# A gated recurrence and a SwiGLU block on one core: two units' decayed k turned through DRAM, sign passes moved between two engines, two outputs on another queue

## The chip, the core and the metric

The kernel runs on one core of one Trainium2 chip. Its engines are TensorE (PE in the profile; PEld is its weight load), VectorE (DVE), ScalarE (ACT), GpSimd (POOL) and SyncE (SP). SyncE, GpSimd and ScalarE can issue DMAs: those of SyncE stand in queue q1, those of GpSimd in q0, those of ScalarE in q10. The metric is the device time of one execution in microseconds, lower being better.

## What is computed

An outer-product recurrence with a decay per channel (4 sequences, 8 heads, 768 steps, 48 channels), whose output is the input of a gated feed-forward block with 384 model and 1536 hidden channels. Cut to what matters:

```python
f = 1.0 / (1.0 + np.exp(-f_logit))
for t in range(S):
    state = f[:, :, t, :, None] * state + np.einsum('bhd,bhe->bhde', k[:, :, t], v[:, :, t])
    y[:, :, t] = np.einsum('bhd,bhde->bhe', q[:, :, t], state)
x = y.transpose(0, 2, 1, 3).reshape(B * S, H * D)
g = x @ w_gate
out = (g * (1.0 / (1.0 + np.exp(-g))) * (x @ w_val)) @ w_out
```

The weights are handed in as 64-bit floats, which the kernel turns into 32-bit ones on the chip.

## The kernel before

**Units and chunks.** Each sequence is cut into 6 chunks of 128 steps. A unit is one chunk of one sequence. Units are numbered chunk by chunk, so that units 0 to 3 are the first chunk (c = 0), 4 to 7 the second, and 8 to 11 the third (c = 2). `attention(u)` is a generator that does one unit, a step at each `next`. After a chunk's four units comes that chunk's feed-forward block. The code runs the block of chunk c while the attention of chunk c + 1 is done.

**One unit.** Sigmoid of f (L619 and L626); f is turned so that channels lie on partitions (L614 by TensorE in the first chunk, L630 by VectorE later); the same for k (L641); `tail`, the decay from a step to the chunk's end, by a scan (L651); the decayed k, kT = k times tail (L593); `gate`, the decay from the start, by a second scan (L681); q turned (L685); qT (L593 again); the scores sc (L700) of kT and qT on TensorE; the mask A (L719) by VectorE; then y (L742 and L746, or L767 with the last sequence) and the chunk's contribution dS (L787) to the state. dS needs the decayed k with the steps on partitions, called kt. There are two ways to it. In one, TensorE transposes kT (L704) and ScalarE copies the result out of PSUM (L717). In the other ("turned"), VectorE transposes blocks of 32 by 32 into the room in which k was loaded (L668), four DMAs write these to DRAM (`turn`, L671), and one DMA reads them back in another order (L709 or L715). In that case the next unit's k (L449), which is loaded into the same room, is asked for only after the turns. Each of its four DMAs fills 32 partitions. In the line of `turned`, the third chunk's first two units go the first way, and the other two the second.

**The blocks.** Chunk 0's block is plain (`mlp_plain`: L836 for gate and val, L859 for the last product). The others (`mlp_fifteen`) take fifteen products (L1052) in place of eighteen in each of four triples, on sums of weights (L951, L954) and of tokens, and seven in place of eight in the last product (L1151, L1214). Each product's accumulator in PSUM is read on the way by ScalarE (`c` or `aside`, L1057) and VectorE (c plus or minus aside or o). Banks named o and c share two buffers, which are also where the second and third unit's scores lie from the third chunk on. The sums of the last product's weights are DMAs that add in flight: ScalarE writes a negated copy (L991), and GpSimd adds to it (L992).

**Weights.** `weight_piece` fetches a piece (L474 by SyncE). ScalarE makes `up` from the low word (L491) and `top` from the high one (L495). VectorE clamps `top` (L505), shifts it and adds (L510 or L516; L502 in the very first, whose two halves are called separately). The sign bits come in one of two ways. For pieces listed in `SIGNED`, ScalarE writes them by a further pass L494, and VectorE shifts only (L508). For the others VectorE shifts and masks (L512) and writes the signs (L514). The first two pieces (gate and val of the first hidden columns) are cut in two halves.

**Order.** The order on TensorE, VectorE, ScalarE and SyncE is written out by hand and pinned by `in_order`; from the third chunk on GpSimd's too. Tables of times (`EARLY`, `CHAINS`, `SCORES`, `JOINS_AT`, `SIZES_AT`, `FETCHES_AT`, `SUMS_AT`, `DOWN_SUMS_AT`) say at which point of the block's products each step of a unit, a piece or a sum is put into that order. An engine takes its instructions strictly in this order: one that waits holds all behind it.

```python
turned = SQUARES * B + 2 <= u < (NCH - 1) * B or c < SQUARES and in_squares
at_once = turned and c >= SQUARES and b < B - 1
```

Here SQUARES is 2 and B is 4, so that the first line begins at unit 10.

Of the kernel before, what the change touches and what calls it, by code (L numbers as in the profile page):

```python
# [290 lines left out]
def short_path(ctx, tc, ident, least, judge, q, k, v, f_logit, moe_w_gate, moe_w_val, moe_w_out, out):  # L291
# [9 lines left out]
    nc = tc.nc  # L301
    B, H, S, D = q.shape
    C = 128
    NCH = S // C
# [11 lines left out]
    SQUARES = 2  # L316
# [86 lines left out]
    def by_squares(u):  # L403
        return u >= SQUARES * B - 3
# [124 lines left out]
    NW = 2  # L529
    FIRST = 2  # L530
    NPART = 2
    SIGNED = (4, 6, 7, 8, 9, 11, 15, 16, 17)

    def add_piece(dst, src, parts=1):
        fetch, *rest = weight_piece(dst, src, parts, len(fetches) in SIGNED)
        fetches.append(fetch)
        for group, fs in zip((sizes, joins), rest):
            group += fs
# [37 lines left out]
    def attention(u):  # L576
        b, c = units[u]
# [7 lines left out]
        in_squares = by_squares(u)  # L585
# [45 lines left out]
            load_after(u, "f")  # L631
        yield

        turned = SQUARES * B + 2 <= u < (NCH - 1) * B or c < SQUARES and in_squares
        turn_queue = nc.sync if c >= SQUARES else nc.gpsimd
        kT = att.tile([128, HP, C], FP32, tag="kT", name="kT")
        qT = att.tile([128, HP, C], FP32, tag="qT", name="qT", bufs=2)
# [8 lines left out]
        n = HP * N1  # L646
# [83 lines left out]
        if c and b < B - 1:  # L730
# [20 lines left out]
            for h in range(H):  # L751
                a, par = h // 2, h % 2
                f = h * D
                while f < (h + 1) * D:
                    n = min((h + 1) * D, (f // 128 + 1) * 128) - f
# [74 lines left out]
    def mlp_plain(c):  # L830
        h = {}

        def product(w, j, name):
            p = fps.tile([128, 512], FP32, tag="m", name=name)[:, 0:TB]
            for i in range(KT):
                nc.tensor.matmul(p, lhsT=w[:, j, i, :], rhs=xT[c][:, i, :],  # L836
                                 start=(i == 0), stop=(i == KT - 1))
            return p

        def part(j):  # L840
            k = 2 * (j // NP)
            return hidden_tile(h, j % NP)[:, k:k + 2, :].rearrange("p a t -> p (a t)")

        def gate(j):
            p = product(w_gate, j, "gate")
            lag(nc.scalar.activation, part(j), p, AF.Silu)

        def val(j):
            p = product(w_val, j, "val")
            lag(nc.vector.tensor_tensor, part(j), part(j), p, ALU.mult)  # L850

        return [*[(PLAIN, lambda j=j, f=f: f(j)) for f, j in ((gate, 0), (val, 0), (gate, 1), (val, 1))],
                *[(PLAIN, lambda j=j, f=f: f(j)) for i in range(2, NF, 2) for f in (gate, val) for j in (i, i + 1)],
                *[(PLAIN_DOWN, f) for f in downs_abreast(c, h)]]
# [48 lines left out]
    def chain(k, q, qmul, turn=None, head=None):  # L903
        return (*[k + t for t in STEPS], turn or k + 3.5, head or k + 3.5, q, qmul)
# [6 lines left out]
        ((PRODUCT - 0.05, "b"), (between[1], "o"), (between[3], "o"), (down[3], "A")),  # L911
        *[((down[10] - whole, "A"), (between[1], "o"), (between[3], "o"), (down[3], "A"))] * (NCH - 4)))}
    CHAINS = {c: chains for c, chains in zip(range(2, NCH), (
        (chain(2.6, 4, 8.6), chain(14.5, 20, 23), chain(30, 37, 43.2), chain(57.4, 57.8, 61)),
        (chain(-12, -8.5, -5), chain(3.5, 6, 9), chain(16, 28, 33, 21.5, 23.5), chain(40.1, 53, 55, 44.5, 52)),
        *[(chain(-19.4, -11.2, -9.5), (-7.5, -6.3, 1.3, 2.2, 3.2, 5.5, 8, 10), chain(16, 28, 33, 21.5, 23.5), chain(40.1, 53, 55, 44.5, 52))] * (NCH - 4)))}
    LAST = 72.5
# [9 lines left out]
    def score_bank(u):  # L927
# [3 lines left out]
            return bank("sc")  # L931
        return {"o": banks_o, "A": banks_a}[kind].tile([128, 512], FP32, tag=kind, name="sc")

    JOINS_AT = (0.8, 4.5, 5, 7.6, 13.2, 16.3, 20.3, 27.2, 29.6, 36.1, 38.7, 43.3, 46.6, 47.8, 55.3, 55.4, 67.6, 70.8)
    SIZES_AT = (0.39, 2.4, 6.2, 11.1, 13.2, 18.4, 18.6, 22.1, 31.8, 38, 39.8, 40.1, 43.1, 50.8, 53, 56, 64.8)
    FETCHES_AT = (-1.1, 0.6, 5.5, 5.9, 6, 9.2, 10.6, 21.1, 23.6, 27, 35.5, 35.5, 37.8, 42.4)
    EARLY = (
        (-1.01, 4.17, 4.58, 9.7, 9.87, 10.5, 11, 11.5, 12, 13.4, 17.3, 22, 28.4, 28.41, 33),
        (26, 31.3, 32.8, 34.3, 34.6, 34.6, 36.1, 37.4, 38.2, 40.6, 43.3, 43.4, 50.8, 54.81, 56),
        (46.2, 49.2, 50.7, 51.4, 51.5, 57, 57.6, 58, 62, 63.9, 64.4, 65.5, 68.2, 68.21, 70),  # L940
        (63, 64, 66.8, 66.9, 67.4, 67.9, 68.6, 71.6, 73.3, 75.9, 76, 76.7, 78, 78.41, 80.3))
    SUMS_AT = (64.3, 64.5, 72.58, 72.7, 74.06, 74.74, 75.3, 75.42, 75.98, 76.02, 76.18, 76.3, 76.66, 76.86,
        77.34, 77.54, 78.22, 78.5, 79.18, 79.86, 81.22, 81.26, 81.26, 81.34, 81.62, 81.9, 81.94, 82.58, 82.58, 82.7,
        83.2)
    LATE_SUMS_AT = (23,)
    FINISH = (3, 5, 6, 7, 9, 10)
    DOWN_SUMS_AT = (5.2, 5.21, 18.8, 18.81, 34.5, 34.51, 43, 43.01)
    sums = {}

    def plus(dst, a, b):  # L950
# [31 lines left out]
    def down_weight_sums():  # L982

        DH = DM // 2
        b11, b12 = w_out[:, 0:NP, 0:DH], w_out[:, 0:NP, DH:DM]
        b21, b22 = w_out[:, NP:NF, 0:DH], w_out[:, NP:NF, DH:DM]
        for i in (1, 2, 4):
            down_sums[i] = comb.tile([128, NP, DH], FP32, tag=f"ws{i}", name=f"ws{i}")
        return [f for dst, a, b in ((down_sums[1], b12, b11), (down_sums[2], b22, down_sums[1]), (b12, b22, b12),
                                    (down_sums[4], b21, down_sums[2]))  # L990
                for f in (lambda dst=dst, b=b: nc.scalar.mul(dst, b, -1.0),  # L991
                          lambda dst=dst, a=a: nc.gpsimd.dma_start(out=dst, in_=a, accum_op=ALU.add))]  # L992
# [10 lines left out]
    def lag(f, *args):  # L1003
        lagging.append(lambda: f(*args))  # L1004
# [123 lines left out]
    def down_seven(c, h):  # L1128
# [15 lines left out]
        def bank2(name, tag):  # L1144
            pool = {"A": banks_a, "B": banks_b, "o": banks_o}[tag]
            return pool.tile([128, 512], FP32, tag=tag, name=name)[:, 0:DM].rearrange("p (n d) -> p n d", n=2)

        def add(p, lhsTs, rhs, first, part):
            for j in order[part * NP // 2:(part + 1) * NP // 2]:
                for n in range(2):  # L1150
                    nc.tensor.matmul(p[:, n, :], lhsT=lhsTs[j][:, n * C:(n + 1) * C], rhs=rhs[:, j, :],  # L1151
                                     start=first and j == order[0] and n == 0, stop=j == order[-1],
                                     skip_group_check=True)

        def of_h(k):
            return [hidden_tile(h, j)[:, k, :] for j in range(NP)]
# [38 lines left out]
        def five(part):  # L1195
            if part == 0:
                kept["p"] = bank2("o7", "o")
            add(kept["p"], of_h(1), b12, True, part)
            if part:
                lag(plus, kept["u"], kept["u"], kept["p"])  # L1200
                lag(plus, kept["o", 1][:, :, DH:DM], kept["u"], kept["p5"])
                lag(plus, kept["o", 1][:, :, 0:DH], kept["u"], kept["p4"])
                for n in range(2):
                    lag(put_out, 1, n, nc.scalar)

        def six(part):
            if part == 0:
# [14 lines left out]
    def in_turn_of_time(waiting, steps):  # L1222

        waiting.sort(key=lambda x: x[0])
        now = 0.0

        def come_in():
            while waiting and waiting[0][0] <= now:
                waiting.pop(0)[1]()

        come_in()
        for took, f in steps:
            come_in()
            before = lagging[:]
            lagging.clear()
            f()
            for g in before:
                g()
            now += took
        come_in()  # L1240
        for g in lagging:
            g()
        lagging.clear()
        assert not waiting
# [4 lines left out]
    mark = traced[-1]  # L1249
    keep_warm(5)  # L1250
    first = [attention(b) for b in range(B)]
    done = [0] * B

    def run(b, *steps):
        for s in steps:
            assert done[b] == s
            done[b] += 1
            for _ in range((3, 1, 5, 3, 3)[s]):
                next(first[b])
# [23 lines left out]
            sizes.pop(0)()  # L1283
        run(b - 1, 4)
    first_join = joins.pop(0)
    first_join(("clamp"))
    sizes.pop(0)()
    run(B - 1, 3)
    first_join(("add"))
    joins.pop(0)()  # L1290
    next(first[B - 1])
    sizes.pop(0)()
# [2 lines left out]

    waiting = [(t, sizes.pop(0)) for t in SIZES_AT]
    waiting += [(t, joins.pop(0)) for t in JOINS_AT]
    waiting += [(t, fetches.pop(0)) for t in FETCHES_AT]
    assert not fetches and not sizes and not joins
    waiting.append((-0.02, lambda: sigmoid_ahead(B)))  # L1300
    for b, at in enumerate(EARLY):
        run_of = attention(B + b)
        waiting += [(t, lambda run_of=run_of: next(run_of)) for t in at]
    sums_of = [weight_sums(odd) for odd in range(2)]
    sums = sums_of[0][0:7] + sums_of[1][0:7] + sums_of[0][7:] + sums_of[1][7:]
    waiting += zip(SUMS_AT, sums[:len(SUMS_AT)])
    in_turn_of_time(waiting, mlp_plain(0))
# [22 lines left out]

    assert len(SUMS_AT) + len(LATE_SUMS_AT) == len(sums)
    waiting += zip(LATE_SUMS_AT, sums[len(SUMS_AT):])
    waiting += [(at, f) for at, f in zip(DOWN_SUMS_AT, down_weight_sums())]
    blocks = {}
# [16 lines left out]
def kernel(  # L1351
# [22 lines left out]
    def judge(bank):  # L1374
# [13 lines left out]
        yield  # L1388

    short_path(tc, ident, least, judge, *args)  # L1390
    with tc.If(redo[0] > 0, label="redo"):
        general_path(tc, *args)
# [32 lines left out]
```

## Time and profile before

| | us |
|---|---|
| Median of 3 runs | 597.67 (597.44 to 597.67) |
| The profiled execution | 597.51 |
| Its span, first to last instruction | 595.8 |
| TensorE busy | 585.5 |
| VectorE busy | 479.3 |
| ScalarE busy | 301.1 |
| GpSimd busy | 112.8 |

The span of the profiled execution leaves out 1.7 us around it. The granted clock of TensorE was 1.0 throughout. The page's slices show where the engines are full: each digit is the busy share of a fortieth of the span, 9 being 90% or more.

```profile
PE   7899999999999999999999999999999999999996
PEld 4744444667888999888999888899988899988896
DVE  7997998999989877998986888994978972666741
ACT  3488677025877322676640667632476730356600
```

VectorE is nearly full in the first third, where it also turns the weights into 32-bit floats and forms their sums. A row of a timeline gives start, duration, engine, line, operation, the tiles written and read, their shapes and the count. What stands in brackets is the idle time before it and what ended that.

### The profile page before, as it was taken

The page shows a single profiled execution, that of the slowest core. Times are in us where ns is not written, and L with a number is a line of the kernel's source. Part 1 is how long each engine was busy: PE and PEld are TensorE (multiplying, and loading weights), DVE is VectorE, ACT ScalarE, POOL GpSimd, SP SyncE. Part 2 cuts the span into 40 slices and gives each one's busy share as a digit, 9 for nine tenths or more (in the row PEclk, how much of TensorE's full clock was granted, in tenths as well). Part 3 has the DMA queues.
Part 4 walks back from the last instruction along what each step waited for, and adds up shares of the span by engine and source line. Part 5 has one row for each costly group of instructions (what it writes and reads, how often), then busy time and mean ns, then how long its engine had stood idle before and what let it go on. Part 6 is the DMA issues. An engine that isn't in the chain of part 4 may idle for free.

```text
span 595.8 us, 10874 instructions
## 1 busy us (share of the span) xinstructions
PE 585.5 (98%) x3972; PEld 481.8 (81%) x3972; DVE 479.3 (80%) x830; ACT 301.1 (51%) x563; POOL 112.8 (19%) x240
## 2 busy tenths in 40 slices
PE   7899999999999999999999999999999999999996
PEld 4744444667888999888999888899988899988896
DVE  7997998999989877998986888994978972666741
ACT  3488677025877322676640667632476730356600
POOL 3140345202132330212030030330030330000000
PEclk9999999999999999999999999999999999999999
DMA  9999487233666565542345332543231100100001
GB/s 205 253 307 286 142 217 186 60 98 107 122 117 110 96 150 136 138 100 64 84 117 137 99 80 62 112 111 99 74 99 28 29 10 6 53 2 1 2 1 56
DMA packets 106291, 61.86 MB, mean 104 GB/s; under 512 B 64200, under 2 KB 97032, under 8 KB 106232
## 3 DMA queue, kind: packets, MB, share of 16 engines
q1 hardware_dynamic: 93800, 45.96, 31.0%
q0 software_dynamic: 10992, 13.19, 10.0%
q10 hardware_dynamic: 1440, 1.97, 0.9%
q8 instruction: 32, 0.52, 0.4%
q14 instruction: 27, 0.22, 0.1%
HBM read 47.64 MB, written 8.13 MB: 94 GB/s over the span
## 4 chain that ended last, share of the span: by engine, by line
PE 98%; DVE 1%; ACT 0%; issue 0%; DVEq 0%
PE o L1151 20%; PE A L1052 18%; PE B L1052 15%; PE c L1052 6%; PE o L1052 6%; PE o L859 5%; PE gate L836 5%; PE val L836 5%; PE sc L700 4%; PE o L1214 3%; PE y L746 3%; PE y L767 2%; PE dS L787 2%; PE y L742 2%; PE kt L704 1%; PE fTp L614 0%
## 5 line engine op out<-in xcount | busy, mean ns | idle before, releaser
L757 POOL DMA_DIRECT2D xT<-yT x120 | 59.8, 506 | 53.4 <-ACT yT L750 49.0
L1052 PE MATMUL A<-xs,w_both 128*128 128x256 f32 x240 | 62.2, 382 | 0.0
L1151 PE MATMUL o<-w_out,h 128*128 128x192 f32 x360 | 62.0, 327 | 0.0
L1151 PEld LDWEIGHTS o<-w_out,h 128*128 128x128 f32 x360 | 58.7, 190 | 1.0 <-issue 0.2
L1057 ACT COPY c<-A 128x512 f32<-128x512 f32 x40 | 23.3, 583 | 60.5 <-PE A L1052 59.4
L1057 ACT COPY aside<-A 128x512 f32<-128x512 f32 x60 | 35.2, 586 | 32.9 <-PE A L1052 32.7
L951 DVE TENSOR_TENSOR c<-c,aside 128x512 f32<-128x512 f32 x60 | 41.1, 685 | 12.8 <-ACT aside L1057 11.1
L1052 PEld LDWEIGHTS A<-xs,w_both 128*128 128x128 f32 x240 | 44.9, 190 | 6.6
L1004 DVE TENSOR_TENSOR h<-h,c 128x256 f32<-128x256 f32 x100 | 40.6, 414 | 7.6 <-ACT h L1068 7.3
L954 DVE TENSOR_TENSOR c<-c,aside 128x512 f32<-128x512 f32 x60 | 41.0, 684 | 2.7 <-ACT aside L1057 2.7
L1068 ACT ACTIVATE h<-c 128x256 f32<-128x256 f32 x100 | 39.4, 417 | 5.0 <-DVE c L951 3.8
L719 DVE TENSOR_TENSOR A<-sc,causal 128x512 f32<-128x512 f32 x48 | 30.9, 685 | 13.4 <-PE sc L700 13.4
L1151 PE MATMUL o<-ws,h 128*128 128x192 f32 x240 | 41.5, 328 | 0.0
L1052 PE MATMUL B<-xs,w_both 128*128 128x256 f32 x160 | 41.3, 380 | 0.0
L1052 PE MATMUL A<-xs,extra 128*128 128x256 f32 x160 | 41.2, 380 | 0.0
L1052 PE MATMUL c<-xT,w_both 128*128 128x256 f32 x160 | 41.1, 379 | 0.0
L1052 PE MATMUL B<-xT,extra 128*128 128x256 f32 x160 | 41.0, 379 | 0.0
L1057 ACT COPY aside<-B 128x512 f32<-128x512 f32 x60 | 35.2, 586 | 9.0 <-PE B L1052 7.0
L1151 PEld LDWEIGHTS o<-ws,h 128*128 128x128 f32 x240 | 39.1, 190 | 0.5
L954 DVE TENSOR_TENSOR c<-o,c 128x512 f32<-128x512 f32 x40 | 27.4, 686 | 11.0 <-ACT h L1068 6.2
L951 DVE TENSOR_TENSOR c<-c,o 128x384 f32<-128x384 f32 x15 | 8.2, 548 | 34.8 <-PE o L1151 34.8
L690 POOL MEMSET gates<- 128x4 f32 x24 | 3.6, 150 | 169.0 <-DVE qT L593 163.9
(163 smaller groups left out, 1240.2 us busy)
## 6 DMA issues: line engine op xcount, KB each, us to landing
fsquares<-in_f_logit_dram SPq DMA_DIRECT2D x64, 96.0 KB, 4.1
qsquares<-in_q_dram SPq DMA_DIRECT2D x64, 96.0 KB, 2.3
ksquares<-in_k_dram SPq DMA_DIRECT2D x64, 96.0 KB, 2.4
w<-in_moe_w_gate_dram SPq DMA_DIRECT2D x6, 768.0 KB
w<-in_moe_w_val_dram SPq DMA_DIRECT2D x6, 768.0 KB, 6.5
w<-in_moe_w_out_dram SPq DMA_DIRECT2D x6, 768.0 KB, 8.8
v<-in_v_dram SPq DMA_DIRECT2D x19, 192.0 KB, 2.8
turn<-ksquares SPq DMA_DIRECT2D x40, 64.0 KB, 2.2
```

The source lines that it names most:

```text
L700: nc.tensor.matmul(sc[par][:, a * C:(a + 1) * C], lhsT=kT[r, a, :], rhs=qT[r, a, :], start=True, stop=True)
L719: nc.vector.tensor_tensor(A[:, par], sc[par].rearrange("p (a t) -> p a t", t=C), causal.unsqueeze(1).broadcast_to((128, HP, C)), ALU.mult)
L757: (nc.gpsimd if c >= SQUARES else nc.sync).dma_start(out=xT[c][f % 128:f % 128 + n, f // 128, b * C:(b + 1) * C], in_=yT[r:r + n, par, a / ...
L836: nc.tensor.matmul(p, lhsT=w[:, j, i, :], rhs=xT[c][:, i, :], start=(i == 0), stop=(i == KT - 1))
L859: nc.tensor.matmul(p, lhsT=hidden_tile(h, n // 2)[:, n % 2 * 2 + b // 2, b % 2 * C:(b % 2 + 1) * C], rhs=w_out[:, j, :], start=(n == 0), s ...
L951: nc.vector.tensor_tensor(dst, a, b, ALU.add)
L954: nc.vector.tensor_tensor(dst, a, b, ALU.subtract)
L1004: lagging.append(lambda: f(*args))
L1052: nc.tensor.matmul(p[name][:, n, :], lhsT=weights_of[a][:, n, j, :], rhs=tokens[b], start=fresh and n == 0, stop=True, skip_group_check=True)
L1057: nc.scalar.copy(t, p[name])
L1068: nc.scalar.activation(dst, src[:, 0, :], AF.Silu)
L1151: nc.tensor.matmul(p[:, n, :], lhsT=lhsTs[j][:, n * C:(n + 1) * C], rhs=rhs[:, j, :], start=first and j == order[0] and n == 0, stop=j == ...
```

## The change

Four things change.

1. Units 8 and 9 go the turned way too: `turned` begins at SQUARES * B. TensorE's L704 and ScalarE's L717 go for both, and VectorE's L668, four DMAs L671 and one read L709 come for each. The loads of k for units 9 and 10 come after the turns of the unit before.
2. `SIGNED` takes in pieces 0 and 1 in place of 4 and 8.
3. The first block of the fifteen-product kind (c = 1) issues its second pair of outputs (`put_out`, L1160) on GpSimd's queue in place of ScalarE's.
4. The tables of times are set anew for the first and second chunk's weight pieces, sums and units, for the third chunk's chains, and for the second pair of the adding DMAs (18.8 becomes 20.7).

The brackets around "clamp" and "add" make tuples of them; the same instructions come out.

```diff
-    SIGNED = (4, 6, 7, 8, 9, 11, 15, 16, 17)
+    SIGNED = (0, 1, 6, 7, 9, 11, 15, 16, 17)
...
-        turned = SQUARES * B + 2 <= u < (NCH - 1) * B or c < SQUARES and in_squares
+        turned = SQUARES * B <= u < (NCH - 1) * B or c < SQUARES and in_squares
...
-        (chain(2.6, 4, 8.6), chain(14.5, 20, 23), chain(30, 37, 43.2), chain(57.4, 57.8, 61)),
+        (chain(2.6, 4.8, 8.6), chain(14.5, 21.7, 23.2, 21.2, 19.6), chain(30, 37, 43.6), chain(57.4, 56.6, 61)),
...
-    JOINS_AT = (0.8, 4.5, 5, 7.6, 13.2, 16.3, 20.3, 27.2, 29.6, 36.1, 38.7, 43.3, 46.6, 47.8, 55.3, 55.4, 67.6, 70.8)
+    JOINS_AT = (0.8, 3.3, 5, 7.6, 12.8, 15.9, 19.9, 22.6, 25.2, 34.9, 38.3, 42.9, 46.6, 48.2, 56.1, 56.2, 67.6, 70.8)
...
-        (-1.01, 4.17, 4.58, 9.7, 9.87, 10.5, 11, 11.5, 12, 13.4, 17.3, 22, 28.4, 28.41, 33),
+        (-1.01, 4.17, 4.58, 9.7, 9.8, 9.87, 11.3, 11.8, 12.3, 14.2, 17.3, 22, 31.4, 31.41, 34.8),
...
-    DOWN_SUMS_AT = (5.2, 5.21, 18.8, 18.81, 34.5, 34.51, 43, 43.01)
+    DOWN_SUMS_AT = (5.2, 5.21, 20.7, 20.71, 34.5, 34.51, 43, 43.01)
...
-                    lag(put_out, 1, n, nc.scalar)
+                    lag(put_out, 1, n, nc.gpsimd if c == 1 else nc.scalar)
...
-    first_join(("clamp"))
+    first_join(("clamp",))
```

## The prediction

> **What bounds the kernel now.** I read the page's chain first, then the waits of TensorE, then the timeline of each engine in three stretches: 22 to 31 us (where TensorE still waits), 28 to 140 us, and 138 to 235 us (the third chunk's attention).
>
> ```profile
> PE 98%; DVE 1%; ACT 0%; issue 0%; DVEq 0%
> ...
> PE idle L362 <- DVE floor L354: 2.1, 1, 2.1
> PE sc L700 <- DVE qT L593: 1.6, 2, 0.8
> ```
>
> The chain that ended last is TensorE for 98% of the span, and what TensorE waits for in the waits view adds up to some 5 us, all of it before 25.3 us. From 29.6 us to the end its starts follow each other without a hole over 0.12 us. So a microsecond can be won in two ways only: by taking matmuls away, or in the opening. It can be lost wherever a wait for TensorE newly appears.
>
> The opening. VectorE clears weights between the last unit's qT and its mask A, and A opens the way to y, xT and the first product:
>
> ```profile
> 25.12 0.70 DVE L505 TENSOR_SCALAR top<-top 128x384 f32<-128x384 f32 x1
> 25.85 0.36 DVE L512 TENSOR_SCALAR top<-top 128x384 int32<-128x384 int32 x1
> 26.13 0.59 DVE L514 TENSOR_SCALAR up<-w 128x384 uint16<-128x384 uint16 x1
> 26.60 1.28 DVE L719 TENSOR_TENSOR A<-sc,causal 128x512 f32<-128x512 f32 x2
> ...
> 25.25 1.16 PE L700 MATMUL sc<-qT,kT 48*128 48x128 f32 x16 [0.79 <-DVE qT L593]
> ```
>
> The transposes to be removed, and for comparison a score step that has none after it:
>
> ```profile
> 150.62 1.16 PE L700 MATMUL sc<-qT,kT 48*128 48x128 f32 x16
> 151.72 0.65 PE L704 MATMUL kt<-idf,kT 128*128 128x128 f32 x4
> 152.21 1.03 PE L1052 MATMUL A<-xT,w_both 128*128 128x256 f32 x4
> ...
> 75.74 1.16 PE L700 MATMUL sc<-qT,kT 48*128 48x128 f32 x16
> 76.83 5.42 PE L836 MATMUL gate<-xT,w_both 128*128 128x512 f32 x12
> ```
>
> VectorE in the third chunk, which has almost no hole from 140 to 169 us: the first unit's kT, the second's k transpose, and the operation that frees the bank which the second unit's scores need.
>
> ```profile
> 144.07 0.66 DVE L593 TENSOR_TENSOR kT<-qT,tails 128x512 f32<-128x512 f32 x1
> ...
> 155.75 0.71 DVE L641 STREAM_TRANSPOSE qT<-ksquares 128x512 f32<-128x512 f32 x1
> ...
> 167.02 0.67 DVE L954 TENSOR_TENSOR c<-c,c 128x512 f32<-128x512 f32 x1
> ...
> 168.73 1.16 PE L700 MATMUL sc<-qT,kT 48*128 48x128 f32 x16
> ```
>
> Last, the DMA queues. The third unit of the chunk already goes through DRAM: its four turn writes, then the next k load, which overwrites what the turns read. GpSimd starts an adding DMA (L992, 576 KB) beside it.
>
> ```profile
> 181.27 2.64 SPq L671 DMA_DIRECT2D turn<-ksquares  x4
> 184.01 6.33 SPq L449 DMA_DIRECT2D ksquares<-in_k_dram  x4
> ...
> 146.64 1.50 POOL L992 DMA_DIRECT2D ws<-w_out  x1 [5.57 <-ACT ws L991]
> 148.50 3.67 SPq L449 DMA_DIRECT2D qsquares<-in_q_dram  x4
> ```
>
> The load that takes 1.8 us to issue elsewhere took 6.33 us. The DMA view of 149 to 152.5 us says why: queue q0 (the adding DMA) moved all 654 packets, SyncE's queue q1 none, though q loads stood in it since 148.50.
>
> **The Trainium skill.** "DMA: Bandwidth & Descriptors", section Issuing engines are not separate DMA queues, says that DMAs from SyncE and GpSimd run on the same 16 engines and interleave. The trace shows the sharing, but not an even one: beside the adding DMA q1 stood still. Its section Queues, rings and completion order has the engines change queues at packet boundaries; that alone would not lead one to expect a q1 at zero, so I take the trace's delay. "VectorE: DVE Perf Modes", section The three transpose paths, says VectorE transposes 32x32 blocks only; that is why L668 needs the way through DRAM. "ScalarE: Activation LUTs", section What ACT_TABLE_LOAD costs, has back-to-back activations overlap by 93 ns; here a 128x768 pass of 1.08 us is followed after 0.94, which agrees, so I count from start to start.
>
> **The change, part by part** (us against before; minus is a gain).
>
> 1. First pieces' signs. On VectorE the join between qT and A becomes L505 and L508 (25.12, then 25.85 to 26.21). A then waits for its scores alone: 25.25 + 1.16 = 26.41 in place of 26.60. y, dS, fTp and the first gate follow: -0.19. ScalarE gets four more passes L494 on 128x384. No row has that shape; its neighbours run 0.5 start to start (0.94 at twice the size, where L494 itself takes 1.0), so 0.53 each, bounds 0.48 and 0.62. Two fall before the xT of the third unit and in the hole at 25.9, harmless. The other two push what follows: second piece pair ready at 37.60 - 0.19 + 1.06 = 38.47, so VectorE reaches the scores' qT at 44.76 + 0.87 = 45.63; TensorE wants it at 46.04 - 0.19 = 45.85. Hidden, by 0.22; at 0.62 a pass it is still hidden, by 0.04. Pieces 4 and 8 lose a pass on ScalarE and cost VectorE 0.5 each; the hole of 4.53 before 60.77 covers them.
> 2. The second chunk's first outputs y move behind one more product; same matmuls, 0. Its DVE order keeps every score's qT ahead of its use.
> 3. kt transposes, units 8 and 9. The step costs 152.21 - 151.72 = 0.49. Without it the next product starts 0.10 slower (5.42 in place of 5.32 after scores). So -0.39 each, -0.78.
> 4. ScalarE loses two kt copies (0.59 each), and L991 moves behind two copies. Two stalls of TensorE, at 158.34 and 162.01 (0.18 and 0.22 with their slower second matmul), which wait for ScalarE's copies, go: -0.40.
> 5. VectorE gets L668 twice, 0.63 start to start. For unit 8 it stands after kT: order and durations give its end at 146.37. qT then ends 149.6, TensorE wants it at 150.43: hidden. The hole of 0.47 at 153.35 takes most; VectorE reaches unit 9's k transpose (L641) at 155.56. For unit 9 nothing takes it: the freeing c operation ends at 168.0 (167.69 - 0.19 - 0.1 + 0.63), where TensorE, with 1, 3 and 4 gained, would start these scores at 167.75. So the scores' second matmul waits 0.3 even if nothing else goes wrong: +0.3. Sum so far -0.19 - 0.78 - 0.40 + 0.3 = -1.07.
> 6. The new wait. SyncE can load unit 9's k only when unit 8's turns have landed, each of four 32-row parts after its own turn. The turns are issued at 146.39, 147.06, 147.73 and 148.40 (0.67 apart as at 181.27). The adding DMA starts at 146.45 and fills the engines from 148.3 to 152.8 (q1 idle from 149.0). A turn's packets move 1.25 after its issue, so the first passes, most of the second and all of the third and fourth stand. About 1390 of 2048 packets are left; q1 moved 1079 of this size in some 1.3 us when alone (DMA view of 226.5 to 228), so they are through at 154.0 and landed at 154.5. The fourth k part is issued then, and lands 2.3 later (median 2.3 around 158 us): 156.8. Before, k had landed long ahead of 155.75. VectorE stops at L641 from 155.56 to 156.85: 1.3. Queued behind are scan, kT, the drains and the freeing c operation; VectorE has no hole before it, so the scores go from 168.05 to 169.35: +1.3. Bounds: 0.5 (turns go as soon as the adding DMA thins, at 151.9) and 2.2 (they crawl as at 188, 160 packets per half us, to the end).
> 7. Unit 9's kt read, the v load, f loads: needed from 174 on, landed by 172 to 175; 0. Outputs by GpSimd's queue: ScalarE's wait at 231 goes, but TensorE has no hole there: 0. GpSimd's next work there is a memset of unit 12's gates at 247.7, so nothing waits for it.
>
> Sum: -1.07 + 1.3 = +0.2. Profiled execution: 597.51 (span 595.8) + 0.2 = 597.7. The median of the runs shown is 597.67, 0.16 above; on it 597.9. The change then comes out even: what its removed transposes win goes back at one DMA wait.
>
> **Rivals.**
> A. The wait of step 6 doesn't come, since the turns slip through ahead of the adding DMA or VectorE arrives later: -1.07; and if VectorE also frees the c bank 0.3 sooner than I count, -1.37. Time 596.3 to 596.6. For it: every piece of the working is a start time to 0.2 us; against it: q1 with no packet for 3.5 us.
> B. Slower: the turns take longer still. The fourth turn at 183.28 let its k load go at 190.0, 6.7 later; here three are stuck in place of one, so 148.40 + 6.7 + 1.0 = 156.1, k landed 158.5, L641 waits 2.9, and the scores come at +1.85 in all: 599.5. It decides from a landing after 157.8 on, where 2.3 of waiting outweighs gains and the limit of 0.2%. Against it: 32 packets per DMA engine and turn, at 20 ns, are soon through once the adding DMA ends.
> C. The signs on ScalarE delay qT at 46 us, by over 0.3: first gain lost, +0.1 to +0.3 more; it stays within the forecast's range.
>
> **From this to the numbers.** 0.2% is 1.2 us, about what a measurement here can tell from no change. Forecast (wait of 0.5 to 2.3, times 597.1 to 598.9, C in it) 0.50, of which 0.05 is over the limit; A 0.28, of which 0.20 beyond -1.2, since its two ends straddle the limit and savings that I rated at nothing would all fall here; B 0.22. Faster 0.20, same 0.53, slower 0.27. The range goes from A's lower end, 596.3, to near B, 599.3.
>
> **What would show it.** Right: A at about 26.4 and the first gate at 29.4; no L704 in the third chunk; SyncE's k load for unit 9 spread over 5 us or more; a VectorE wait of about 1.3 us before L641 near 156 for a DMA; unit 9's scores at about 169.3. Wrong: L641 without a wait (A), or unit 9's scores after 170 (B); a hole on TensorE at 46 us would put step 1 wrong, one near 176 us step 7.

## The result, and the profile after

| | before | changed |
|---|---|---|
| Median, us | 597.67 (597.44 to 597.75, 6 runs) | 600.20 (600.01 to 600.89, 6 runs) |
| Span of the profiled execution | 595.8 | 598.3 |

The ratio is 1.0045, with an interval of 1.0033 to 1.0058: slower by 2.5 us, where 0.2 was forecast and 599.3 was the range's end. Both spans differ by the same 2.5.

The waits view of the changed kernel, first for TensorE, then for VectorE. The columns are us in total, times, longest.

```profile
PE B L1052 <- ACT aside L1057: 0.8, 1, 0.8
...
PE c L1052 <- DVE c L954: 0.5, 1, 0.5
PE c L1052 <- ACT c L1057: 0.4, 1, 0.4
...
PE B L1052 <- ACT c L1057: 0.3, 1, 0.3
```

```profile
DVE qT L641 <- DMA ksquares<-in_k_dram: 3.4, 2, 3.0
```

TensorE, which had no such holes before, has four, all for banks that other engines free. VectorE's transposition of k (L641) waits for its load twice, once for 3.0 and once for 0.4. The timelines say where. This is TensorE of the changed kernel from 158 to 175 us.

```profile
160.22 1.13 PE L1052 MATMUL c<-xT,w_both 128*128 128x256 f32 x4 [0.45 <-DVE c L954]
...
162.55 1.13 PE L1052 MATMUL B<-xs,w_both 128*128 128x256 f32 x4 [0.34 <-ACT c L1057]
164.09 1.13 PE L1052 MATMUL c<-xT,w_both 128*128 128x256 f32 x4 [0.41 <-ACT c L1057]
...
166.88 1.13 PE L1052 MATMUL B<-xT,extra 128*128 128x256 f32 x4 [0.80 <-ACT aside L1057]
...
170.87 1.55 PE L700 MATMUL sc<-qT,kT 48*128 48x128 f32 x16
172.35 1.13 PE L1052 MATMUL A<-xs,w_both 128*128 128x256 f32 x4
```

Unit 9's scores come at 170.87 in place of 168.73, and the product after them at 172.35 in place of 170.31, 2.04 late although a transposition step went in between. What holds the four products begins with one wait of VectorE, and SyncE's own timeline shows where that comes from: the k load for unit 9, asked from 149.11, takes 6.79 us to issue, since each part may only follow its own turn.

```profile
158.86 0.73 DVE L641 STREAM_TRANSPOSE qT<-ksquares 128x512 f32<-128x512 f32 x1 [2.98 <-DMA ksquares<-in_k_dram]
```

```profile
146.37 2.64 SPq L671 DMA_DIRECT2D turn<-ksquares  x4
149.11 6.79 SPq L449 DMA_DIRECT2D ksquares<-in_k_dram  x4
```

The chain of waits of the same kernel, asked from 150 to 172 us (start, us, what), ties the pieces together. It begins with the fourth turn, issued at 148.38.

```profile
148.38 7.14 DMA turn<-ksquares
...
155.59 3.15 DMA ksquares<-in_k_dram
...
158.86 0.06 DVE qT L641
...
159.50 0.66 DVE c L954
160.16 1.14 DVE tails L651
...
163.45 0.58 ACT c L1057
...
164.88 1.06 ACT ws L991
...
166.25 0.58 ACT aside L1057
...
166.88 1.13 PE B L1052 x4
```

The fourth turn takes 7.14 us to land, the k part that waits for it 3.15 more, and only then do L641 and the drains behind it move (drains are the operations of VectorE and ScalarE that empty TensorE's PSUM banks). ScalarE, now late as well, meets its negated copy of 1.06 (L991) just ahead of the `aside` that TensorE waits for.

### The profile page after: what moved, and what is told of

Its sections match the earlier page's. It is cut to its first block, busy times and chain, and to the rows that moved or that the text cites. A ratio compares the mean times of both kernels' runs of the same rounds, so it can differ in the third digit from the quotient of the medians.

```text
span 598.3 us, 10872 instructions
## 1 busy us (share of the span) xinstructions
PE 586.2 (98%) x3964; PEld 481.4 (80%) x3964; DVE 480.1 (80%) x830; ACT 300.4 (50%) x563; POOL 113.4 (19%) x242
## 4 chain that ended last, share of the span: by engine, by line
PE 94%; DMA 2%; DVE 2%; ACT 1%; issue 0%; SPq 0%; DVEq 0%; ACTq 0%
PE o L1151 20%; PE A L1052 17%; PE B L1052 14%; PE o L1052 6%; PE o L859 5%; PE gate L836 5%; PE val L836 5%; PE c L1052 5%; PE sc L700 4%; PE o L1214 3%; PE y L746 3%; PE y L767 2%; PE dS L787 2%; PE y L742 1%; DMA turn<-ksquares 1%; DMA ksquares<-in_k_dram 1%
```

## The experiments

My theory, T in the expectations: unit 8's turns share the DMA engines with the first adding DMA (L992, 146.65), k of unit 9 therefore lands late, and all of the loss comes through that. The others: VectorE has too much to do (R1), the new tables, signs or output queue cost the time (R2). Every ratio below is to the kernel before, measured beside it on the same chip.

**The adding DMAs moved out of the way.** In both, nothing but GpSimd's order changes: the adding DMA goes behind the next gate memset.

```diff
-    DOWN_SUMS_AT = (5.2, 5.21, 20.7, 20.71, 34.5, 34.51, 43, 43.01)
+    DOWN_SUMS_AT = (5.2, 9.5, 20.7, 20.71, 34.5, 34.51, 43, 43.01)    # the first alone
+    DOWN_SUMS_AT = (5.2, 9.5, 20.7, 23.5, 34.5, 34.51, 43, 43.01)     # both
```

> The first adding DMA (L992) alone is issued one GpSimd instruction later, after unit 8's gate memset: about 149.5 in place of 146.65. Theory T (unit 8's turns stand behind that adding DMA, so unit 9's k lands late and L641 holds VectorE for 3.0 us): the turns land by about 150.5, the fourth k part by about 153, L641 starts at 155.8 without a wait, unit 9's scores at about 168 in place of 171.1, time 596.5 to 597.3. Rival R1 (VectorE has simply too much to do in 140 to 170 us once two L668 and the turned order are in, the wait only stands where the delay would show anyway): scores of unit 9 at 170 or later and 599.3 or more. Rival R2 (the new tables of times or the signs cost the time): 600.0 to 600.4, as the changed kernel.

> As the run with the first adding DMA later, and the second one too is issued after unit 9's gate memset, about 168.5, so that unit 9's turns (issued from about 162.6) are also through before it. T: the same gain as the run before, and the load of unit 10's k no longer spread over 6.8 us; if step 7's hole near 176 was of this second collision, another 0.1 to 0.4 less: 596.3 to 597.0. R1: 599 or more. If the second collision costs nothing, within 0.15 of the run with only the first moved.

Measured: 597.50 with the first alone, ratio 0.9998 (0.9989 to 1.0006), level with the kernel before and above the expected range; and 596.81 with both, ratio 0.9986 (0.9979 to 0.9993), faster than either kernel. SyncE and then VectorE with both moved:

```profile
146.40 2.64 SPq L671 DMA_DIRECT2D turn<-ksquares  x4
149.13 1.99 SPq L449 DMA_DIRECT2D ksquares<-in_k_dram  x4
```

```profile
155.78 0.73 DVE L641 STREAM_TRANSPOSE qT<-ksquares 128x512 f32<-128x512 f32 x1
```

The same four turns at the same moment, and the load behind them issues in 1.99 in place of 6.79. L641 starts at 155.78 without a wait, 3.08 earlier than in the changed kernel; the product after the scores starts at 169.28, 3.07 earlier. The wait went to TensorE one for one. R1 and R2 fall: all the work and all the tables are still there.

With only the first moved, unit 9's turns (from 162.50) still meet the second adding DMA (163.50). VectorE of that run:

```profile
175.82 0.73 DVE L641 STREAM_TRANSPOSE qT<-ksquares 128x512 f32<-128x512 f32 x1 [1.59 <-DMA ksquares<-in_k_dram]
```

It is the same event one unit later: 1.59 of waiting, 0.7 us by the medians, 1.5 by the two spans (596.4 and 594.9; this run's profiled execution, 598.11, was 0.6 above its median). It is why the first move alone missed its range. In the changed kernel the same meeting cost 0.4 of waiting.

**Which unit's turns.** The changed kernel with fewer turned units.

```diff
-        turned = SQUARES * B <= u < (NCH - 1) * B or ...
+        turned = SQUARES * B + 2 <= u < (NCH - 1) * B or ...                        # neither
+        turned = SQUARES * B + 1 <= u < (NCH - 1) * B or ...                        # only unit 9
+        turned = SQUARES * B <= u < (NCH - 1) * B and u != SQUARES * B + 1 or ...   # only unit 8
```

> The changed kernel with units 8 and 9 again the first way (transposed by TensorE, copied by ScalarE); signs, outputs' queue and tables stay. T: the loss goes and the front's gain of 0.17 stays; 597.1 to 597.8 (0.1 to 0.5 less than before, or even with it). R2 (tables, signs or queue cost the time): 599 or more. R1: as T here.

> The changed kernel with only unit 9 turned; unit 8 goes the first way, so unit 9's k is loaded without waiting for turns. T: L641 of unit 9 does not wait for a DMA, one transposition step (0.39) is saved, unit 9's turns still meet the second adding DMA: 596.8 to 597.4. R1 (each L668 costs its 0.63 or more on TensorE): 598 or more.

> The changed kernel with only unit 8 turned (unit 9 goes the first way). T (all of the loss begins with unit 8's turns and the first adding DMA): L641 of unit 9 still waits some 3.0 for its k, unit 9's transposes are back (+0.4), unit 10's wait of 0.4 is gone: 600.0 to 600.7. Rival R5 (the two turned units are needed together, the loss comes from the second collision): 597.5 or less.

Measured: neither 597.84, ratio 0.9999 (0.9991 to 1.0007); only unit 9 597.54, 0.9996 (0.9988 to 1.0005); only unit 8 600.47, 1.0047 (1.0032 to 1.0062). The loss comes with unit 8's turns and stays without unit 9's. In that run L641 waits 3.33 before 159.90. Signs, queue and tables by themselves are worth nothing that this measurement can see, though 0.17 was expected to stay; the section on the steps says where it went. The first two times lie just above their expected ranges. With only unit 9 turned, L641 waits for no load, and VectorE's last copy starts at 590.60 in place of 591.04, so the saved transposition is there in the trace; the medians don't show it, and the profiled span is no shorter (596.0).

**Is it the move by itself?** The kernel before, with its two adding DMAs moved in the same way.

```diff
-    DOWN_SUMS_AT = (5.2, 5.21, 18.8, 18.81, 34.5, 34.51, 43, 43.01)
+    DOWN_SUMS_AT = (5.2, 9.5, 18.8, 23.5, 34.5, 34.51, 43, 43.01)
```

> Control: the kernel before, with the same two adding DMAs issued one GpSimd instruction later as in the run with both later. T (the move helps only since it takes the adding DMAs out of the way of the new turns): the kernel before has no turns there, so 597.5 to 597.9, no change. Rival R4 (the move itself is what gained, with or without the turns): about 596.8.

Measured: 597.55, ratio 0.9999 (0.9991 to 1.0007). The move is worth something only beside the turns.

**Ahead of the turns instead of behind them.**

```diff
-    DOWN_SUMS_AT = (5.2, 5.21, 20.7, 20.71, 34.5, 34.51, 43, 43.01)
+    DOWN_SUMS_AT = (0.4, 0.41, 20.7, 23.5, 34.5, 34.51, 43, 43.01)
```

> The changed kernel with the first adding DMA earlier (about 141.3 in place of 146.65), so that it is through at about 148.5, and the second one later as before. T (only the overlap in time counts, not which of the two is asked first): k of unit 9 lands by 154, L641 does not wait, 596.7 to 597.3. If an adding DMA that is asked ahead of the turns holds them whatever the times are: L641 waits over 1 and 598 or more. ScalarE's negated copy (1.17) now stands between two copies that free banks, which may cost up to 0.3 at 141 to 143.

Measured: 596.57, ratio 0.9982 (0.9975 to 0.9989). The adding DMA is issued at 141.47, the k load takes 1.99 to issue and L641 starts at 155.84 without a wait. The time is a little better than expected. Either order will do, as long as the two don't overlap.

**Late turns, but a k that doesn't wait for them.** L668 of units 8 and 9 writes into the room of the hidden sums (hs, not in use until 187), so that k for the next unit is asked for at once. The adding DMAs stay where they are.

```diff
+        own_room = c == SQUARES and b < 2
...
-            if not turned:
+            if not turned or own_room:
                 load_after(u, "k")
...
-            beside = rooms["k"][:, 0:HP * C].rearrange("p (i m) -> p i m", i=NI)
+            room = hs_rooms[c - 1][b].rearrange("p n t -> p (n t)") if own_room else rooms["k"]
+            beside = room[:, 0:HP * C].rearrange("p (i m) -> p i m", i=NI)
...
-            load_after(u, "k")
+            if not own_room:
+                load_after(u, "k")
```

> The changed kernel with both adding DMAs where they are (146.65, and the second one after unit 9's turns are asked), but L668 of units 8 and 9 writes into a room of its own (that of the hidden sums, free until 187), so that the loads of k for units 9 and 10 are asked right after the k transposition L641 before, ahead of the turns. T (the loss goes only by k, turns and adding DMA may be as slow as they like: q and kt are wanted much later): k of unit 9 lands before 150, L641 does not wait, 596.5 to 597.0, as with the adding DMAs moved. Rival R7 (the slow turns also cost by another way, the read of kt or the q load, or VectorE and TensorE are slowed by the DMAs' traffic itself): 597.6 or more.

Measured: 596.84, ratio 0.9980 (0.9971 to 0.9989). SyncE and VectorE of that run, whose line numbers are one to four higher from L641 on:

```profile
143.81 1.80 SPq L449 DMA_DIRECT2D ksquares<-in_k_dram  x4
146.96 2.64 SPq L673 DMA_DIRECT2D turn<-hs  x4
149.70 5.20 SPq L449 DMA_DIRECT2D qsquares<-in_q_dram  x4
```

```profile
156.35 0.72 DVE L642 STREAM_TRANSPOSE qT<-ksquares 128x512 f32<-128x512 f32 x1
```

Here the overlap is still there: a turn takes up to 7.4 us to land, and the q loads behind the turns take 5.20 to issue. Nothing is lost by it, since q is wanted only at 165. So the loss needs both: the overlap, and a load that is wanted within 10 us and may only follow the turns. R7 falls: the DMAs' traffic by itself costs VectorE and TensorE nothing that this measurement can see.

**L641 later in VectorE's order.** If k comes late, let the drains go first.

```diff
-        (chain(2.6, 4.8, 8.6), chain(14.5, 21.7, 23.2, 21.2, 19.6), ...
+        (chain(2.6, 4.8, 8.6), chain(17, 21.7, 23.2, 21.2, 20.4), ...
```

> The changed kernel, its adding DMAs as they are, with unit 9's steps on VectorE asked for later: the k transposition L641 behind four of the feed-forward block's drains, wanted at about 158.5 in place of 155.8. T (what costs is that VectorE's strict order holds the drains behind L641, while TensorE waits for the banks they free): k lands at 158.7 as before, L641 waits under 0.5, the holes of TensorE at 160 to 167 shrink, and unit 9's scores come at 168 to 169.3: 597.0 to 598.5. Rival R6 (unit 9's own chain, k to kT to the scores, is what is late, and the drains are not): scores at 171 and 600 or more.

Measured: 601.00, ratio 1.0054 (1.0038 to 1.0069), slower still. My expectation failed. TensorE of that run:

```profile
164.75 1.13 PE L1052 MATMUL B<-xT,extra 128*128 128x256 f32 x4 [0.36 <-ACT aside L1057]
...
170.37 1.66 PE L700 MATMUL sc<-qT,kT 48*128 48x128 f32 x16 [1.55 <-DVE qT L593]
171.96 1.63 PE L1052 MATMUL A<-xs,w_both 128*128 128x256 f32 x4
173.38 1.91 PE L1052 MATMUL B<-xs,w_both 128*128 128x256 f32 x4
```

One half of it held: with the drains ahead of L641 three of the four holes between 160 and 167 are gone. But L641 still waited 1.44 (to 159.27), the whole chain from k to qT was then as late as in the changed kernel, and the scores waited for it in one piece at 170.37. R6 had the scores nearly right. It was not the scores that made this run slower, though: the product after them starts at 171.96, ahead of the changed kernel's 172.35. Then four matmuls take 1.63 and 1.91 in place of 1.03, and four products on, the same work starts at 177.20 in place of 175.91; the last section has the clock.

**Getting more out of it.** The late weight sum (w_both, 0.60 on VectorE) goes behind the operation that frees unit 9's bank, first with both adding DMAs later, then with the first one ahead of the turns.

```diff
-    LATE_SUMS_AT = (23,)
+    LATE_SUMS_AT = (25.9,)
```

> The run with both adds later, and the late weight sum (w_both, 0.60 from start to start) goes behind VectorE's operation that frees the c bank of unit 9's scores. If VectorE's order still sets the scores' start (they waited for the c operation at 168.2, and two TensorE holes before it for ScalarE's asides), the scores come up to 0.5 earlier and the time is 596.3 to 596.7. If TensorE's own order sets it, 596.8 as in that run.

> The run with the first adding DMA ahead of the turns, and the late weight sum behind the operation that frees unit 9's bank: 596.2 to 596.6, 0.1 to 0.2 less than that run, as the late sum gave 0.1 to 0.2 with the other placing.

Measured: 596.59, ratio 0.9984 (0.9976 to 0.9991), and 596.68, ratio 0.9985 (0.9978 to 0.9991). With both adding DMAs later, the unit's scores shrink from 1.23 to 1.16 and the next product starts at 169.19 in place of 169.28: 0.1 in the trace, not to be told apart by the times. With the first one ahead of the turns, the expected further gain didn't come (596.68 after 596.57, above the range). These four versions (596.57 to 596.81), and the one with a k that doesn't wait (596.84), are about 1 us faster than the kernel before and 3.5 faster than the changed one.

**The signs alone**, on the kernel before.

```diff
-    SIGNED = (4, 6, 7, 8, 9, 11, 15, 16, 17)
+    SIGNED = (0, 1, 6, 7, 9, 11, 15, 16, 17)
```

> The kernel before with the signs of pieces 0 and 1 in place of 4 and 8 by ScalarE, nothing else. Step 1's arithmetic: A at 26.4, TensorE 0.15 to 0.19 earlier from 27 on. If that gain lasts to the end: 597.4 to 597.6; if it goes at the o bank at 140.1 as in the changed kernel: 597.6 to 597.8. If ScalarE's two further passes hold the first block's products (rival C): 598 or more.

Measured: 597.60, ratio 1.0 (0.9991 to 1.0009). This can't tell: in its profiled execution (599.81) the opening's loads came late and TensorE ran 1.2 us behind from 27 us on. What it shows is that A waits for its scores alone (0.24 idle, released by L700), and that nothing of rival C's 598 comes.

## Why the prediction was wrong, step by step

"Before", "after" and "both later" are the start times of the same TensorE work in three traces. A product that follows scores directly, or a wait, starts early but takes 1.10 to 1.13 for its four matmuls in place of 1.03, so the table has the product behind it.

| | before | after | both later |
|---|---|---|---|
| y of the fourth unit (L767) | 27.39 | 27.23 | 27.24 |
| product after the `o` product of 140 us | 141.03 | 141.05 | 141.06 |
| second product after unit 8's scores | 153.07 | 152.69 | 152.71 |
| second product after unit 9's scores | 171.18 | 173.32 | 170.25 |
| first `o` product after unit 10's k | 185.13 | 187.61 | 184.19 |
| end of the span | 595.8 | 598.3 | 594.9 |

Step 1, the signs, came as worked out at its place: the first gate at 29.47 (forecast 29.43), the scores of 46 us at 45.89 without a wait. That the gain lasts was wrong. At 140 us it is used up. VectorE of the changed kernel shows a likely reason:

```profile
139.12 0.42 DVE L951 TENSOR_TENSOR xT<-xT 128x256 f32<-128x256 f32 x1
139.46 0.55 DVE L880 COPY ob<-o 128x384 f32<-128x384 f32 x1
```

Half of a token sum now stands ahead of the copy that empties an `o` bank; before, it stood behind it. The copy ends at 140.01 and the `o` product starts at 140.11, takes 1.10 in place of 1.03, and what follows starts no earlier than before (141.05, 141.03). That the order is the cause was read, not tried.

Step 2 cost nothing that shows. Step 3 holds: the first transposition step gave 0.38. Step 4 holds at its two places (with both later, 0.18 and 0.22 come back at 158 and 162), but a new small stall for an `aside` at 164.1 takes 0.16 of it again. Step 5's wait at the scores is 0.07 (they take 1.23 in place of 1.16) rather than 0.3. With both adding DMAs out of the way TensorE stands at 170.25 - 171.18 = -0.93, where the sum of steps 1 to 5 said -1.07. That it came so near is in part luck: steps 1, 4 and 5 were off by some 0.2 each, two of them one way and one the other. One reading of the prediction is loose: a ScalarE pass of 1.08 followed after 0.94 overlaps by 0.14, half as much again as the 93 ns with which it was said to agree. Nothing rests on that, since the passes were counted from start to start.

Step 6 is the step that failed, by size: a wait of 1.3 was forecast and 2.98 measured, above the upper bound of 2.2. On TensorE it cost 173.32 - 170.25 = 3.07, which is 1.77 more than forecast and most of the 2.3 by which the whole forecast was short. The mechanism was right, the time to land was not. Its terms:

| | forecast | measured |
|---|---|---|
| fourth turn landed | 154.5 | 155.53 |
| fourth k part, from issue to landing | 2.3 | 3.15 |
| k landed | 156.8 | 158.74 |

The first term rests on a picture: the turns stand still until the adding DMA is through at 152.8, then run at full rate. The prediction had it from the view of 149 to 152.5 us, in which q loads stand beside the adding DMA, not turns. Where turns do stand beside one in the trace of before, from 185 to 188 us, it is nearly so (packets, MB, share of the 16 engines):

```profile
q0 software_dynamic: 671, 0.51, 126.6%
q1 hardware_dynamic: 20, 0.00, 1.1%
```

The changed kernel shows something else, first from 149 to 151 us, then from 151 to 152.5:

```profile
q0 software_dynamic: 375, 0.29, 113.9%
q1 hardware_dynamic: 134, 0.02, 10.3%
```

```profile
q0 software_dynamic: 251, 0.19, 112.9%
q1 hardware_dynamic: 238, 0.03, 26.5%
```

The turns don't stand, they crawl, and at the end the two queues go nearly packet for packet. That last is what the Trainium skill ("DMA: Bandwidth & Descriptors", section Queues, rings and completion order) leads one to expect of engines that change queues at packet boundaries, if its packets are what the view counts; 375 to 134 and 671 to 20 are far from it, and what sets the share stays open. Packet for packet is little for a turn: its packet carries 0.03 MB / 238, about 128 bytes, the adding DMA's 0.19 MB / 251, about 760. The adding DMA is late too. It landed at 155.18, 8.5 us after its issue, in place of 7.1 in the kernel before, so that the turns did not have the engines to themselves from 152.8 on, and the fourth landed at 155.53. Without an adding DMA beside it a turn lands 2.2 after its issue, as the DMA view of 147.5 to 150 with both moved has it (KB each, median us to landing):

```profile
turn<-ksquares SPq DMA_DIRECT2D x3, 64.0 KB, 2.2
```

Step 7 rated what follows the turns at nothing, which is wrong too: unit 9's turns met the second adding DMA (166.25), and unit 10's L641 waited 0.44 for its k. Until then TensorE is 3.07 later than with both later, and after it 187.61 - 184.19 = 3.42: another 0.35.

The sum with the measured terms: -0.93, +3.07 for the first wait and +0.35 for the second give +2.49, against 2.5 in the spans.

Rival B had the mechanism and nearly the numbers: k at 158.5 (158.74), a wait of 2.9 (2.98). It was worked out from a case in the trace of before in which a turn had met an adding DMA, 6.7 us from issue to landing (7.14 here); the forecast preferred a count of packets over that. That the numbers agree so well is part luck: B had the fourth turn land at 156.1 (155.53) and k 2.4 later (3.15), and the two errors cancel. It still came out 0.7 too fast, half of it since it left the second collision's 0.35 out.

## What to carry to other kernels

When a change puts a DMA ahead of a load, ask what else is in the queues at that minute, and how many packets it has: here a turn of small packets took 7.1 us beside a large transfer and 2.2 without. If the trace before holds one instance of such a meeting, take its duration, not an arithmetic that assumes one of the two unhindered. And a chain that loses should be read back to its first link before the idea is dropped: here one line of times, or another buffer, turned 2.5 us lost into 1 us won.

## What was not expected of the hardware

In the run with L641 later, a hole of 1.55 us on TensorE was followed by some 4 us at a lower granted clock. The windows view of that run, then of the one with both adding DMAs later, from 172 to 176.5 us (busy us of each engine and instructions, then PEclk, DMA share, GB/s):

```profile
172.00:176.50 4.50, 4.50 (x14) 3.69 (x14) 1.84 (x5) 1.73 (x3) 3.92 (x8) 0.62 0.89 220
```

```profile
172.00:176.50 4.50, 4.50 (x22) 3.96 (x21) 4.26 (x8) 4.01 (x9) 1.12 (x3) 1.00 1.11 198
```

14 matmuls in place of 22. At the full clock four of them begin within 0.86 us, so the 8 missing ones are 1.7 us. The Trainium skill ("TensorE: Matmul & The Clock Gate", section Part 1: The HAM clock gate) has the clock fall after an idle window of some 3.4 us. In this run no hole between 158 and 172 us is that long; the longest is the 1.55. It is hardly one execution's chance: the mean clock was 0.997 in all four runs of this kernel, and 0.998 to 1.00 in nearly all others. That the hole is the cause was not tried. The changed kernel's holes of 0.3 to 0.8 left the clock at 1.00, and so did one of 1.33 before 9.88 us.

The opening varies from execution to execution with the landing of the first loads: TensorE's y of the fourth unit started between 27.2 and 27.9 in most traces and at 28.6 in that with the signs alone. An effect of 0.2 us in a single profile is therefore to be read only from starts inside a stretch, not from the span.
